# Leaving 24 unseen keys of the preceding block out of local attention, with masks made ahead of the counts

## The chip, the cores and the metric

The kernel runs on one core of one Trainium2 chip. The metric is device time in microseconds (us) of one execution. The kernel before takes 615.64 us (median of three runs, 615.52 to 617.7). The engines are called as in the profile: PE (matrix multiply; PEld is its weight load), DVE (vector), ACT (scalar), POOL, and SP, which here only issues DMA transfers.

## The reference

Attention with a local window of 96 keys, 8 global keys and a linear distance bias, followed by a feed-forward layer with a sigmoid gate. There are 4 batches of 8 heads and 768 positions, in float32.

```python
batch, n_heads, seq, head_dim = (4, 8, 768, 64);  n_global, n_local = (8, 96)
scores = scale * np.matmul(q, k.transpose(0, 1, 3, 2))
rel = pos[:, None] - pos[None, :]
is_global = pos[None, :] < int(n_global)
is_local = (rel >= 0) & (rel < int(n_local))
keep = is_global | is_local
dist = np.where(is_global & ~is_local, float(n_local), np.abs(rel).astype(np.float32))
scores = np.where(keep, scores + bias, -1000000000.0)      # bias = -slope of the head * dist
a = np.exp(scores - max);  a = a / (sum(a) + 1e-09)
x = np.matmul(a, v)                                         # to [3072 tokens, 512]
h = x @ w_in                                                # 512 -> 2048
return (h * (1.0 / (1.0 + np.exp(-1.702 * h)))) @ w_out     # 2048 -> 512
```

## The kernel before

**Blocks.** Queries are worked through in 24 blocks of 128 positions. A block's queries see keys of their own block and of the one before it, so the scores of one head are 128 x 256: 128 columns of the preceding block, then 128 of the own one. The 8 global keys are written over columns 0 to 31 (`NG = 32`) of the preceding block's keys, which are too far away for any query of this block; a mask leaves out the rest. The first block of each of the four batches (blocks 0 to 3) has no preceding one and goes another way (`first`, L555).

**A unit** (`unit`, L497) is two heads of a block: eight matmuls of 128 x 128 give the scores (L513; float32 values are carried as a high and a low half in 16 bit, hence two products for each), DVE adds the mask and takes the maximum (L519), ACT the exponential (L529), ACT and DVE split the result into halves `hl` (L533, L534), a DMA transposes them to `pt` (L535), and twelve matmuls with 64 columns multiply them with the values (L544 to L546). There are 80 units.

**The feed-forward layer** goes over 12 chunks of two blocks. Chunks 0 to 2 use plain products (L762, 128 x 256), the first two interleaved; from chunk 3 (`TWO`) on seven half products take the place of eight (L802). The products with `w_out` are L870. All 16 weight tiles (`w` followed by step and 0 for `w_in`, 1 for `w_out`) come as raw 8-byte numbers; each takes a DMA of 1 MB to one of three buffers `ws`, two ACT operations (L364, L365), two DVE (L362, L366), one ACT (L367) and one DVE (L368). Chunk 0 needs the first of them early on, so the first 80 us hold the weights, the masks and the first blocks at once.

**Masks.** `places` (POOL) writes positions, `counts` (DVE) turns n_local and n_global to numbers, `own` and `other` (DVE) make three 128 x 128 patterns `mk` out of them, and `slopes` scales each by the eight heads to `mm`: first the one for blocks 0 to 3 (task `M1`, L334 on 128 x 128), then the two for the units (`M2`, L334 on 128 x 256).

**The order of the work** is set by a planner in the kernel (`Work.order`, L94). Each task has costs by engine, tasks that it waits for, buffers from rings, and a due time; the planner goes through time and gives each free engine the ready task that is due first, not earlier than `AHEAD` us before it is due. What it writes down is the fixed sequence of each engine, SP included: engines run their own sequence in order and wait for each other by semaphores. Where PE would have nothing to do in the first `WARM` us, spare matmuls on a constant tile (`idle`, L1028) are put in. `T0`, `PACE0` and `SKEW` set the due times of chunks 0 and 1 (L900).

## Time and profile before

| what | value |
|---|---|
| three runs | 615.64 us median (615.52 to 617.7) |
| the profiled execution's own time | 614.86 us |
| its span, first to last instruction | 613.0 us |
| outside the span | 1.86 us |
| PE busy | 589.7 us (96%) |
| DVE, ACT busy | 507.5 us (83%), 485.0 us (79%) |
| granted TensorE clock, mean | 0.996 |
| DMA moved | 112.59 MB, mean 184 GB/s |

A busy PE is a modelled figure, since its matmuls overlap: each lasts longer than the time until the next one starts, so the pace is read from start to start. A view by stretches shows where PE lacks work; the waits show which engine it lacked it from; the timeline shows single instructions with their start and duration.

### The profile page before, as it was taken

To read this page: it belongs to the slowest core of one execution; us is meant where nothing else is said; L and a number is where in the kernel's file an instruction comes from. 1 tells how busy PE (TensorE), PEld (TensorE's weight loads), DVE (VectorE), ACT (ScalarE), POOL (GpSimd) and SP (SyncE) were. 2 spreads that over 40 slices of the span, in tenths; PEclk is the share of its full clock that TensorE was granted. 3 is DMA by queue.
4 is the path that set the end of the run, shared out by engine and by line. 5 is a ranking of instruction groups with operands and counts; after the bars stand their busy time and mean duration, and the time that the engine had idled before them with its cause. 6 is when DMAs were issued, how large, how long until landed. Compare 5 with 4: busy or idle time off the path is not lost.

```text
span 613.0 us, 17039 instructions
## 1 busy us (share of the span) xinstructions
PE 589.7 (96%) x6798; PEld 443.3 (72%) x6798; DVE 507.5 (83%) x1170; ACT 485.0 (79%) x1101; POOL 3.9 (1%) x16
## 2 busy tenths in 40 slices
PE   7978999999999999999999999999999999999996
PEld 4866667776776677677877668767777777867795
DVE  5699899999999999888879889879979887857533
...
GB/s 200 259 264 274 238 295 225 217 206 198 189 128 175 164 78 167 203 189 190 201 219 187 181 229 205 219 234 223 198 239 204 203 210 226 198 37 1 36 1 40
DMA packets 275670, 112.59 MB, mean 184 GB/s; under 512 B 256000, under 2 KB 256512, under 8 KB 275584
## 3 DMA queue, kind: packets, MB, share of 16 engines
...
q10 hardware_dynamic: 288, 0.00, 0.0%
HBM read 57.67 MB, written 6.29 MB: 104 GB/s over the span
## 4 chain that ended last, share of the span: by engine, by line
PE 50%; DVE 19%; DMA 12%; ACT 10%; issue 6%; SPq 1%; DVEq 0%; POOL 0%; ACTq 0%; POOLq 0%
PE y L870 22%; PE pa L802 10%; PE pb L802 7%; DMA QK<-qk 3%; DMA pt<-hl 3%; PE s L513 3%; DVE p L519 2%; ACT p L529 2%; PE h L762 2%; DVE hl L534 2%; DMA QK<-QK 2%; DVE t L772 1%; DMA ws_01again<-in_moe_w_in_dram 1%; DVE t L708 1%; ACT junk L394 1%
## 5 line engine op out<-in xcount | busy, mean ns | idle before, releaser
L870 PE MATMUL y<-w,g 128*128 128x512 f16 (+1 forms) x1248 | 268.0, 363 | 2.8 <-DVE g L774 2.0
L870 PEld LDWEIGHTS <-g 128*128 128x128 f16 x1248 | 117.7, 98 | 106.3 <-DVE g L774 3.0
L802 PEld LDWEIGHTS <-w 128*128 128x128 f16 x1728 | 101.7, 98 | 6.8 <-issue 2.1
L529 ACT ACTIVATE p<-p,NM 128x256 f32<-128x256 f32 x160 | 79.7, 501 | 6.9 <-DVE NM L519 6.7
L802 PEld LDWEIGHTS <-T 128*128 128x128 f16 x1296 | 77.0, 98 | 5.8 <-issue 0.7
L762 PE MATMUL h<-xT,w 128*128 128x256 f16 x576 | 70.1, 274 | 0.5 <-DVE w L368 0.5
L519 DVE CUSTOM_DVE_ANT_0 p<-s,mm 128x256 f32<-128x256 f32 x160 | 61.4, 420 | 7.4 <-PE s L513 6.5
L762 PEld LDWEIGHTS <-w 128*128 128x128 f16 x576 | 55.6, 99 | 10.9 <-DVE w L368 0.7
L534 DVE TENSOR_TENSOR hl<-p,hl 128x512 f16<-128x512 f32 x80 | 55.0, 688 | 9.4 <-ACT hl L533 9.0
L843 DVE SCALAR_TENSOR_TENSOR g<-t,g 128x512 f16<-128x512 f32 x72 | 49.2, 688 | 9.4 <-ACT g L842 9.0
L834 ACT ACTIVATE t<-h 128x512 f32<-128x512 f32 (+1 forms) x72 | 36.3, 518 | 24.6 <-DVE h L810 22.1
L842 ACT ACTIVATE g<-t 128x512 f16<-128x512 f32 x72 | 44.9, 629 | 9.4 <-DVE t L835 9.3
L533 ACT CAST hl<-p 128x512 f16<-128x512 f32 x80 | 49.3, 616 | 2.5 <-DMA pt<-hl 0.6
L810 DVE TENSOR_TENSOR h<-pb,h 128x256 f32<-128x256 f32 x72 | 29.5, 420 | 23.6 <-PE pb L802 20.5
L835 DVE SCALAR_TENSOR_TENSOR t<-t,h 128x512 f32<-128x512 f32 (+1 forms) x72 | 38.7, 554 | 8.1 <-ACT t L834 7.7
L802 PE MATMUL pa<-xS,T 128*128 128x128 f16 x648 | 45.0, 219 | 0.4 <-ACT h L818 0.4
L513 PEld LDWEIGHTS <-QK 128*128 128x128 f16 x640 | 39.2, 98 | 6.4 <-DVE NM L519 2.5
L513 PE MATMUL s<-QK 128*128 128x128 f16 x320 | 40.0, 219 | 0.8 <-DMA QK<-QK 0.8
L802 PE MATMUL pb<-xS,w 128*128 128x128 f16 x540 | 37.5, 219 | 1.7 <-ACT h L807 1.7
L802 PE MATMUL pa<-xT,w 128*128 128x128 f16 x540 | 37.2, 219 | 0.0
L544 PE MATMUL pv<-VR,pt 128*128 128x64 f16 x288 | 35.0, 193 | 1.1 <-DMA pt<-hl 1.1
L545 PE MATMUL pv<-VR,pt 128*128 128x64 f16 x288 | 35.0, 193 | 0.0
(184 smaller groups left out, 1076.5 us busy)
## 6 DMA issues: line engine op xcount, KB each, us to landing
...
```

The source lines that it names most:

```text
L513: nc.tensor.matmul(sp()[:, j, s * P:(s + 1) * P], d["QK"]()[:, 0, h, :], K[:, 1 + z, h, :], start=(z == 0), stop=(z == 1), skip_group_chec ...
L519: nc.vector.tensor_tensor_reduce(out=pr()[:, j, :], in0=sp()[:, j, :], in1=m, scale=-1.0 / SC, scalar=3.0e38, op0=ALU.add, op1=ALU.min, ac ...
L529: ex.append(add({"ACT": 0.28 + 0.105 * ns}, lambda e, j=j: nc.scalar.activation(pr()[:, j, :], pr()[:, j, :], AF.Exp, bias=NM[:, n, hs[j]: ...
L533: t4 = add({"ACT": 0.1 + 0.215 * ns}, lambda e: nc.scalar.copy(hl()[:, 0], pr()), ex, [pr, hl])
L534: t5 = add({"DVE": 0.07 + 0.265 * ns}, lambda e: nc.vector.tensor_sub(hl()[:, 1], pr(), hl()[:, 0]), [t4], [pr, hl])
L762: nc.tensor.matmul(ph()[:, fi, :], w1(s, cc, z, fi), X[:, y, cc, :], start=(j + cc == 0), stop=(j == 2 and cc == NCC - 1))
L802: nc.tensor.matmul(o()[:, fi], w, x()[:, y * NCC + 2 * k + cc, t], start=(first and fi + j + cc == 0), stop=(last and j + cc == 3), skip_g ...
L834: t1 = add({"ACT": 0.06 + 0.22 * w}, lambda e: nc.scalar.activation(o(), src(), AF.Tanh, scale=0.851 / (SX * SW)), after, srcs)
L835: return add({"DVE": 0.08 + 0.265 * w}, lambda e: nc.vector.scalar_tensor_tensor(o(), o(), 1.0, src(), ALU.add, ALU.mult), [t1], srcs)
L842: t4 = add({"ACT": 0.53}, lambda e, g=g, tt=tt: nc.scalar.mul(g()[:, 0], tt(), SG / (SX * SW)), u, [tt, g])
L843: t5 = add({"DVE": 0.61}, lambda e, g=g, tt=tt: nc.vector.scalar_tensor_tensor(g()[:, 1], tt(), SG / (SX * SW), g()[:, 0], ALU.mult, ALU.s ...
L870: nc.tensor.matmul(y(), part(zg, f), w2(s, z, f % 2)[:, m], start=(begin and f + j == 0), stop=(end and j == 2 and f == 2 * len(steps) - 1 ...
```

## The change

The 24 columns 0 to 23 (`SKIP = 24`) of the preceding block are left out. With 96 local keys no query sees a preceding key below column 33, so the 8 global keys now take columns 24 to 31 (`NG = 8`), and scores, masks' sum, exponential and halves work on 232 columns in place of 256. Of a unit's eight score matmuls, the four on the preceding block have 104 columns. The transpose to `pt` and the products with the values keep all 256: the two `hl` tiles are now fixed tiles, whose 24 unused columns are set to zero once (`clear`).

The copies of global keys and values are shorter, and the handover at the start of a batch copies them in place too (`lead_keys`). Masks: the part that needs no counts (`distances`) comes first, and `own` and `other` are fewer operations; the zeroing of `mT` goes from POOL to DVE. The second half of the scores of blocks 0 to 3 gets a buffer of its own kind (ring `h` in place of `s`). The planner's costs and due times are other ones.

```diff
+NG = 8
+SKIP = 24
-AHEAD = 25.0
+AHEAD = 20.0
...
-        nc.gpsimd.memset(t, 0.0)
+        nc.vector.memset(t, 0.0)
...
+    r_hl.tiles = [const.tile([P, 8 * P], F16, name=f"hl{j}") for j in range(2)]
...
+    def distances(e):
+        nc.vector.tensor_copy(flt()[:, 0:2], ints())
+        nc.vector.tensor_copy(id16, ident)
+        nc.vector.tensor_scalar(mk()[:, 1], rel(), 0.0, -BIG, ALU.is_lt, ALU.mult)
+        nc.vector.tensor_sub(mk()[:, 1], mk()[:, 1], rel())
+        nc.vector.tensor_scalar(mk()[:, 0], rel(), -1.0, float(-P), ALU.mult, ALU.add)
...
     def own(e):
-        nc.vector.tensor_scalar(nnl, nl, -1.0, None, ALU.mult)
-        nc.vector.tensor_scalar(a_(), rel(), nl, None, ALU.is_lt)
-        nc.vector.scalar_tensor_tensor(a_(), rel(), 0.0, a_(), ALU.is_ge, ALU.mult)
-        local(mk()[:, 1], 0.0)
-        nc.vector.scalar_tensor_tensor(a_(), col(), ng, a_(), ALU.is_lt, ALU.is_gt)
-        nc.vector.tensor_copy(mk()[:, 2], mk()[:, 1])
-        nc.vector.copy_predicated(mk()[:, 2], a_().bitcast(I32), nnl.broadcast_to([P, P]))
+        nc.vector.tensor_scalar(a_(), rel(), nl, -BIG, ALU.is_ge, ALU.mult)
+        nc.vector.tensor_add(mk()[:, 1], a_(), mk()[:, 1])
+        nc.vector.tensor_scalar(b_(), col(), ng, -BIG, ALU.is_ge, ALU.mult)
+        nc.vector.scalar_tensor_tensor(mk()[:, 2], b_(), nl, mk()[:, 1], ALU.subtract, ALU.max)
...
+        d["VG"] = [add({"SP": 0.3}, lambda e: nc.sync.dma_start(d["VR"]()[SKIP:SKIP + NG], d["VR"]()[0:NG]), d["v_ready"], [d["VR"]])]
...
-        W = ns * P
+        W = ns * P - SKIP
...
-                        nc.tensor.matmul(sp()[:, j, s * P:(s + 1) * P], d["QK"]()[:, 0, h, :], K[:, 1 + z, h, :],
+                        lo, hi = (0, P - SKIP) if s == 0 else (P - SKIP, W)
+                        nc.tensor.matmul(sp()[:, j, lo:hi], d["QK"]()[:, 0, h, :], K[:, 1 + z, h, P - (hi - lo):],
...
+        t4 = add({"ACT": 0.5}, lambda e: nc.scalar.copy(hl()[:, 0, :, SKIP:], pr()), ex, [pr, hl])
+        t5 = add({"DVE": 0.55}, lambda e: nc.vector.tensor_sub(hl()[:, 1, :, SKIP:], pr(), hl()[:, 0, :, SKIP:]), [t4], [pr, hl])
...
-            sp = Buf(r_s, [P, 4, P], F32, f"s{n}_{f}")
+            sp = Buf((r_s, r_h)[f], [P, 4, P], F32, f"s{n}_{f}")
...
-    T0, PACE0, PACE, PACE2, LAG, SKEW, LEAD = 20.0, 6.0, 5.9, 5.7, 16.0, 3, 68.0
+    T0, PACE0, PACE, PACE2, LAG, SKEW, LEAD = 25.0, 7.0, 5.9, 5.7, 16.0, 4, 68.0
...
-            first(n, 8.0 + 10.0 * n)
+            first(n, 8.0 + 8.0 * n)
```

Since the planner runs on these figures, the sequences of all engines move. Three places matter for the prediction.

The first is DVE at the start: `counts`, `own`, the masks of blocks 0 to 3 (`mm` 128x128 x8) and the maxima `top` of block 0. Before:

```order
L314 TENSOR_SCALAR flt_148<-flt_148,cnt_68 128x128
L315 SCALAR_TENSOR_TENSOR flt_148<-flt_148 128x128
L290 TENSOR_SCALAR flt_148<-flt_148 128x128
L291 SCALAR_TENSOR_TENSOR mk_167<-flt_148 128x128
L292 TENSOR_TENSOR mk_167<-flt_148,mk_167 128x128
L317 SCALAR_TENSOR_TENSOR flt_148<-flt_148,cnt_68 128x128
L318 COPY mk_167<-mk_167 128x128
L319 COPY_PREDICATED mk_167<-flt_148,nnl_90 128x128
L334 TENSOR_SCALAR mm_89<-mk_167 128x128 x8
```

Now:

```order
L306 SCALAR_TENSOR_TENSOR cnt_68<-cnt_68,cf_67 128x2
L319 TENSOR_SCALAR flt_123<-flt_123,cnt_68 128x128
L320 TENSOR_TENSOR mk_126<-flt_123,mk_126 128x128
L321 TENSOR_SCALAR flt_123<-flt_123,cnt_68 128x128
L322 SCALAR_TENSOR_TENSOR mk_126<-flt_123,cnt_68,mk_126 128x128
L335 TENSOR_SCALAR mm_91<-mk_126 128x128 x8
L422 TENSOR_SCALAR QZ1_133<-tq1_0_181 64x4x128
L325 TENSOR_SCALAR flt_123<-mk_126,cnt_68 128x128
L326 SCALAR_TENSOR_TENSOR mk_126<-flt_123,mk_126 128x128
L327 TENSOR_SCALAR mk_126<-flt_123,cnt_68 128x8
```

Four operations stand between the counts and the scaled mask in place of nine, three in place of seven make the other pattern, and the eight 128 x 256 scalings of the units' masks have left DVE for ACT. DVE takes over two conversions of blocks 0 and 1 from ACT (`QZ1`, and the keys of block 1).

The second is SP, after the raw weights `ws0_1`: transposes to `QK2` and `QK3` (queries and keys of blocks 2 and 3), raw weights `ws`, values `VF`. Before:

```order
L448 DMA_TRANSPOSE QK2_307<-qk162_0_270 128x16x128
L196 DMA ws1_0_335<-in_moe_w_in_dram 128x4x512
L196 DMA ws1_1_380<-in_moe_w_out_dram 128x2x1024
L450 DMA QK2_307<-QK2_307 64x1024 x2
L196 DMA ws2_0_419<-in_moe_w_in_dram 128x4x512
L448 DMA_TRANSPOSE QK3_438<-qk163_0_401 128x16x128
L431 DMA VF2_123<-in_v_dram 128x8x64
L431 DMA VF3_383<-in_v_dram 128x8x64
L196 DMA ws2_1_511<-in_moe_w_out_dram 128x2x1024
```

Now:

```order
L451 DMA_TRANSPOSE QK2_334<-qk162_0_296 128x16x128
L201 DMA ws1_0_367<-in_moe_w_in_dram 128x4x512
L201 DMA ws1_1_399<-in_moe_w_out_dram 128x2x1024
L453 DMA QK2_334<-QK2_334 64x1024 x2
L451 DMA_TRANSPOSE QK3_422<-qk163_0_406 128x16x128
L434 DMA VF2_224<-in_v_dram 128x8x64
L201 DMA ws2_0_478<-in_moe_w_in_dram 128x4x512
L453 DMA QK3_422<-QK3_422 64x1024 x2
L201 DMA ws2_1_520<-in_moe_w_out_dram 128x2x1024
```

The load of `ws2_0` has gone behind the transpose for block 3 and the values of block 2.

The third is DVE around the weight tile `w4_0`, which the fifth product of chunk 0 needs. Before:

```order
L366 ISA wa3_1_761<-wa3_1_761,w3_1_765 128x2048
L362 TENSOR_SCALAR wa4_0_827<-ws4_0_717 128x1024
L674 TENSOR_TENSOR x163_811<-x3_791,x163_811 128x512
L366 ISA wa4_0_827<-wa4_0_827,w4_0_813 128x2048
L772 SCALAR_TENSOR_TENSOR t0_3_837<-t0_3_837,h0_3_795 128x512
L368 SCALAR_TENSOR_TENSOR w3_1_765<-wa3_1_761,w3_1_765 128x1024
L446 SCALAR_TENSOR_TENSOR qk16over4_1_849<-over4_752,qk16over4_1_849 128x8x64
L368 SCALAR_TENSOR_TENSOR w4_0_813<-wa4_0_827,w4_0_813 128x1024
```

Now:

```order
L369 ISA wa3_1_758<-wa3_1_758,w3_1_740 128x2048
L369 ISA wa4_0_784<-wa4_0_784,w4_0_786 128x2048
L789 SCALAR_TENSOR_TENSOR g0_2_823<-t0_2_765,g0_2_823 128x512
L689 TENSOR_TENSOR x163_827<-x3_806,x163_827 128x512
L787 SCALAR_TENSOR_TENSOR t0_3_832<-t0_3_832,h0_3_789 128x512
L371 SCALAR_TENSOR_TENSOR w3_1_740<-wa3_1_758,w3_1_740 128x1024
L371 SCALAR_TENSOR_TENSOR w4_0_786<-wa4_0_784,w4_0_786 128x1024
L789 SCALAR_TENSOR_TENSOR g0_3_854<-t0_3_832,g0_3_854 128x512
L449 SCALAR_TENSOR_TENSOR qk164_0_845<-raw4_731,qk164_0_845 128x16x64
```

The two conversions for block 4 (`qk164` and `qk16over4`) stood ahead of `w4_0` and now stand behind it. On PE the scores of block 4's units come later as well: three of them (`s4_0`, `s4_1`, `s4_2`) now follow each other with nothing in between.

73 lines of the change are left out of this document (38 added, 35 removed).

## Prediction

> **What bounds the kernel now.** I read the stretches first, to see where PE, the busiest engine, lacks work. The columns are the stretch, its length, then busy us of PE, PEld, DVE, ACT and POOL with instruction counts, and the granted clock.
>
> ```profile
> core 0: us, PE busy (x) PEld busy (x) DVE busy (x) ACT busy (x) POOL busy (x), PEclk, DMA share, GB/s
> 0.00:20.00 20.00, 16.23 (x86) 9.64 (x87) 12.93 (x48) 8.93 (x11) 3.89 (x16) 1.00 0.90 216
> 20.00:40.00 20.00, 17.62 (x158) 15.81 (x158) 13.84 (x26) 14.71 (x16) 0.00 (x0) 0.91 1.05 255
> 40.00:60.00 20.00, 15.96 (x177) 13.20 (x175) 18.98 (x28) 17.06 (x24) 0.00 (x0) 1.00 1.02 275
> 60.00:80.00 20.00, 18.75 (x130) 12.56 (x129) 17.25 (x25) 18.10 (x24) 0.00 (x0) 1.00 1.12 254
> 80.00:140.00 60.00, 60.00 (x549) 43.31 (x548) 57.14 (x112) 57.43 (x111) 0.00 (x0) 1.00 1.08 231
> 140.00:240.00 100.00, 95.89 (x1083) 69.94 (x1082) 95.51 (x212) 80.95 (x192) 0.00 (x0) 1.00 0.83 157
> 240.00:600.00 360.00, 357.03 (x4556) 271.87 (x4554) 289.11 (x714) 285.19 (x724) 0.00 (x0) 1.00 0.87 173
> 600.00:613.00 13.00, 8.26 (x77) 6.95 (x74) 2.80 (x11) 2.65 (x7) 0.00 (x0) 0.93 0.15 47
> ```
>
> From 80 to 600 us PE is idle for 0 + 4.1 + 3.0 = 7.1 us of 520. The first 80 us hold 3.8 + 2.4 + 4.0 + 1.3 = 11.4 us of idle PE. The other engines matter where they make PE wait: in the first 80 us, and between 140 and 240 us, where DVE is busy for 95.5 of 100. So the end moves by PE's own work, by idle PE in the front, and by the 7.1 us behind it; DVE and ACT work that is saved elsewhere is hidden behind PE.
>
> That PE's busy time is its pace must be checked, since the durations overlap. The timeline shows starts (column one) and durations (column two):
>
> ```profile
> 341.27 0.19 PE L544 MATMUL pv<-VR,pt 128*128 128x64 f16 x1
> 341.30 0.19 PE L545 MATMUL pv<-VR,pt 128*128 128x64 f16 x1
> 341.32 0.19 PE L546 MATMUL pv<-VR,pt 128*128 128x64 f16 x1
> 341.35 0.28 PE L513 MATMUL s<-QK,QK 128*128 128x128 f16 x2
> 341.69 0.28 PE L513 MATMUL s<-QK 128*128 128x128 f16 x2
> 341.80 1.03 PE L870 MATMUL y<-w,g 128*128 128x512 f16 x4
> ```
>
> A matmul with 64 columns takes 0.029 us from start to start, one with 128 columns 0.056 (eight from 341.35 to 341.80). That is 0.42 ns a column and about 2 ns besides.
>
> **The change, part by part.** *Score columns.* The matmuls on the preceding block are these two groups of the view by lines, with shapes kept apart (count, then busy us and mean ns):
>
> ```profile
> L513 PE MATMUL s<-QK,QK 128*128 128x128 f16 x256 | 32.0, 219 | 1.5 <-DVE NM L519 1.3
> L513 PE MATMUL s<-QKover,QK 128*128 128x128 f16 x64 | 8.0, 219 | 0.0
> ```
>
> 320 matmuls lose 24 columns each: 320 x 24 x 0.42 ns = 3.3 us, all of it PE work and nearly all of it in the stretches where PE is never idle. The bounds are 0 (something other than the columns sets the pace) and 3.3; I take 3.3, since the 64-column rows show the pace following the columns well below 104. The Trainium skill ("TensorE: Matmul & The Clock Gate", section "Back-to-back issue gap") speaks against this: in a stream of weight loads and matmuls it has the spacing set by both, at about 81 ns for 128 columns, and by that rule shorter matmuls behind whole weight loads would save nothing. The trace does not agree: 56 ns at 128 columns and 29 ns at 64, each matmul with its load.
>
> *DVE and ACT in the units.* The same view:
>
> ```profile
> L519 DVE CUSTOM_DVE_ANT_0 p<-s,mm 128x256 f32<-128x256 f32 x160 | 61.4, 420 | 7.4 <-PE s L513 6.5
> L534 DVE TENSOR_TENSOR hl<-p,hl 128x512 f16<-128x512 f32 x80 | 55.0, 688 | 9.4 <-ACT hl L533 9.0
> L529 ACT ACTIVATE p<-p,NM 128x256 f32<-128x256 f32 x160 | 79.7, 501 | 6.9 <-DVE NM L519 6.7
> L533 ACT CAST hl<-p 128x512 f16<-128x512 f32 x80 | 49.3, 616 | 2.5 <-DMA pt<-hl 0.6
> L807 ACT COPY h<-pa 128x256 f32<-128x256 f32 x36 | 13.4, 371 | 3.1 <-PE pa L802 3.1
> ```
>
> DVE goes from 420 ns at 256 columns to 688 at 512, 1.05 ns a column: 160 x 24 + 80 x 48 columns are 7680, 8.0 us of 507. ACT by 371 and 616 is 0.96 ns a column: 7.4 us of 485. PE hides all of this from 240 us on. Between 140 and 240 us, where DVE is nearly full, there lies about a fifth of the units: 0.2 x 8.0 = 1.6 us, against 4.1 us of idle PE. I take 1.0 us off; bounds 0 and 1.6. The shorter copies of global keys and the four more small DMAs of the handovers lie far ahead of their use; I charge nothing, and 1 us if one of the handover's is late.
>
> *Masks and the first blocks.* The timeline of DVE and PE at the start, three rows of SP, and the first product of chunk 0:
>
> ```profile
> 6.51 0.69 DVE L419 TENSOR_SCALAR QZ<-tq 64x512 f32<-64x512 f32 x1 [5.55 <-ACT QZ L419]
> 7.57 0.16 DVE L297 CAST cf<-ci 128x4 f32<-128x4 int32 x1
> 8.44 0.28 DVE L314 TENSOR_SCALAR flt<-flt,cnt 128x128 f32<-128x128 f32 x1
> 8.75 0.29 DVE L315 SCALAR_TENSOR_TENSOR flt<-flt 128x128 f32<-128x128 f32 x1
> 10.65 1.17 DVE L334 TENSOR_SCALAR mm<-mk 128x128 bf16<-128x128 f32 x8
> 13.50 0.69 DVE L583 TENSOR_REDUCE top<-s 128x4 f32<-128x512 f32 x1
> 14.11 1.70 DVE L334 TENSOR_SCALAR mm<-mk 128x256 bf16<-128x256 f32 x8
> 15.83 0.69 DVE L583 TENSOR_REDUCE top<-s 128x4 f32<-128x512 f32 x1
> 16.66 0.46 PE L578 MATMUL s<-KF,QZ 128*128 128x128 f32 x2 [0.44 <-DVE top L583]
> 18.01 0.27 PE L586 MATMUL aux<-ident,top 128*8 128x128 f32 x1
> 28.21 0.38 SPq L196 DMA_DIRECT2D ws<-in_moe_w_in_dram  x1
> 33.74 3.05 SPq L448 DMA_TRANSPOSE QK<-qk  x1
> 36.84 1.95 SPq L431 DMA_DIRECT2D VF<-in_v_dram  x2
> 36.45 3.42 PE L762 MATMUL h<-xT,w 128*128 128x256 f16 x24
> ```
>
> The scaled mask of block 0 is there at 11.8 us. Now the casts and `distances` lie in DVE's 5.6 us of waiting ahead of `QZ`; behind its end at 7.2 stand four counts (0.8 us, as from 7.57 to 8.37), four 128 x 128 operations at the 0.31 of 8.44 to 8.75 (1.2) and the scaling (1.2): 10.4, 1.4 us earlier. The scores need 2 x 1.3 us (16.66 to 18.01 is one half), and the second half no longer waits for the maximum of the first; nor does the scaling of 14.11 stand ahead of its maximum. So both maxima are taken by about 13.7 in place of 16.5, and `aux` of block 0 comes at about 13.8 in place of 18.0. Behind it the same chain runs. The eight scalings on ACT, at most 8 x 0.37 = 3.0 us by the 371 ns row, start behind the other pattern at about 11.7 and end by 14.7, 0.6 us behind `aux`; ACT's 11 us of idleness in the first 20 cover them. Following block 0 and 1 with the same durations, the first product of chunk 0 comes about 4 us before 36.45.
>
> How much of this reaches the end is decided later, at the last wait for DVE before PE fills up:
>
> ```profile
> 70.10 1.22 DVE L368 SCALAR_TENSOR_TENSOR w<-wa,w 128x1024 f16<-128x1024 f32 x1
> 71.38 0.83 PE L762 MATMUL h<-xT,w 128*128 128x256 f16 x6 [0.46 <-DVE w L368]
> ```
>
> This is `w4_0`, ready at 71.3, and the second half of the fifth product of chunk 0 waiting for it. In the new sequence PE has the same work ahead of that product (the same scores, values and products of chunk 0, in another order, less what stands behind it in both). So the front gains what `w4_0` gains. Two conversions for block 4 leave DVE's queue ahead of it, one of 1024 columns, by the view by lines,
>
> ```profile
> L446 DVE SCALAR_TENSOR_TENSOR qk<-raw,qk 128x1024 f16<-128x1024 f32 x22 | 26.8, 1220 | 2.2 <-ACT qk L445 2.2
> ```
>
> and one of 512 (0.69, as `hl` above): 1.9 us. The scalings (1.7), five mask operations more than come in (at 0.31, 1.6) and a small cast (0.3) leave too, 5.5 us in all; two conversions of 0.69 like `QZ` and small fills (0.4) come in, 1.8. Net 3.7 us. Against it: the raw load of `w2_0` was issued at 28.21 and now stands behind the transpose for block 3. That was issued by 36.8 and may now be some 2 us earlier; with one load of values (1.0, half of 1.95) `w2_0` is issued at about 36, 8 us later. PE asks for it behind 5.8 us more of its own work (scores of block 3 and the first products with `w_out`), and DVE can meanwhile do other tiles, but not for all of it. I take 3.0 us for the front. The ends are 6 (the 4 us of the chain and half of the 3.7) and -5 (the late load passes on to `w4_0`).
>
> *New stalls.* `s4_0`, `s4_1` and `s4_2` follow each other directly on PE; each needs the score buffer back from two additions on DVE. The wait list of before has this wait:
>
> ```profile
> PE s L513 <- DVE NM L519: 1.3, 1, 1.3
> ```
>
> Twice 1.3 would be 2.6 us, of which the place may have some anyway by waiting for weights; I take 1.5, bounds 0 and 2.6. The fixed `hl` tiles keep the two-deep ring and so its waits.
>
> The sum on the profiled execution: 614.9 - 3.3 - 1.0 - 3.0 + 1.5 = **609.0 us** (609.1, rounded). Its 614.86 lies 0.8 below the median of 615.64, so the median could come out that much higher.
>
> **The rivals.** *The front is given back* (0.18). The late load of `w2_0` eats the 3.0 us and the stalls stay: 614.9 - 3.3 - 1.0 + 1.5 = 612.1. For it speaks that DVE and ACT are at 17 to 19 of 20 us from 40 us on; against it that DVE has less to do ahead of `w4_0`.
>
> *The columns save nothing* (0.05): 609.0 + 3.3 = 612.3. The 64-column rows speak against it. The rule of the skill named above is this one.
>
> *The front carries through* (0.08). All 6 us and no stall at `s4`: 614.9 - 3.3 - 1.0 - 6.0 = 604.6, and less than that if the half clock in the 0.91 of 20 to 40 us (0.09 x 20 = 1.8 us) goes with it.
>
> *Slower* (0.09): `w4_0` becomes the place where the program is late. PE cannot pass the fifth product of chunk 0 without it, and behind it PE has nothing idle to catch up with until 140 us. If block 3's transpose is no earlier, `w2_0` is issued at 36.8 + 1.0 = 37.8, 9.6 us late; if the ring of three raw buffers hands this on undiminished but for DVE's 3.7 us, `w4_0` is ready at 71.3 + 9.6 - 3.7 = 77.2, 5.9 later; with 2.6 of stalls: 614.9 - 3.3 + 5.9 + 2.6 = 620.1. It decides from a readiness of about 74 us on, since 71.3 + 3.3 pays for the columns. DMA at a share of 1.02 to 1.12 in that time speaks for it; that every later load (`ws3_0` on) stands earlier relative to block 4's transfers speaks against it.
>
> *The change does not do what it says* is excluded for the columns, since the new sequence has 104-column matmuls; for the masks it is the first rival.
>
> **How the numbers follow.** The forecast has 0.60. What can be told from no change in this kernel is about 0.5%, 3.1 us: faster means below 612.6, slower above 618.7. Faster: the forecast, the front that carries through, 0.10 of the first rival and 0.02 of the second: 0.80. Slower: 0.08, nearly all of the last rival. The rest, 0.12, is no difference. The range reaches from the case in which the front carries through and the clock goes with it (about 602) to past the two rivals near 612 with the median's 0.8 and 1 us for a late handover: 602 to 614.5.
>
> **What would show it.** The score matmuls on the preceding block at 0.046 us from start to start, the others at 0.056. PE's idle time from 240 to 600 us at 3 us or less. `aux` of block 0 near 14 us and the first product of chunk 0 near 32. `w4_0` ready near 68; if it is at 71 the front was given back, if beyond 74 the kernel is slower. PE waiting for DVE between `s4_0` and `s4_2`. The prediction is wrong if PE's idle time behind 80 us grows by more than 3 us, at a place that I did not name.

## The result and the profile after

The changed kernel takes 607.84 us (median of four runs, 605.45 to 609.57); the kernel before took 616.52 beside it. The ratio is 0.9849, with a 95% interval of 0.9822 to 0.9876 (the quotient of the two medians, 0.9859, lies inside it). The profiled execution has a time of 606.97 us and a span of 605.1 us, 7.9 us less than the 613.0 before. Both profiled executions are among the quicker ones of their kernels; the one before took 614.86 us, 1.7 less than the median beside the changed kernel. In the comparison of the experiments below the same kernel came out at 608.67 us, ratio 0.9878 (0.986 to 0.9897).

The view by stretches of the changed kernel, with the columns of the first view of the prediction:

```profile
core 0: us, PE busy (x) PEld busy (x) DVE busy (x) ACT busy (x) POOL busy (x), PEclk, DMA share, GB/s
0.00:20.00 20.00, 16.71 (x116) 12.20 (x117) 13.05 (x39) 10.71 (x18) 3.68 (x14) 1.00 0.97 223
20.00:40.00 20.00, 17.46 (x152) 13.64 (x152) 15.35 (x27) 14.41 (x18) 0.00 (x0) 1.00 1.00 235
40.00:60.00 20.00, 17.97 (x183) 14.31 (x181) 18.05 (x30) 18.39 (x22) 0.00 (x0) 1.00 1.04 319
60.00:80.00 20.00, 19.66 (x144) 13.75 (x143) 19.02 (x26) 20.00 (x26) 0.00 (x0) 1.00 1.00 269
80.00:140.00 60.00, 56.81 (x499) 38.72 (x497) 55.22 (x111) 51.35 (x102) 0.00 (x0) 0.97 0.99 201
140.00:240.00 100.00, 97.48 (x1141) 72.24 (x1141) 95.87 (x225) 80.14 (x192) 0.00 (x0) 1.00 0.88 157
240.00:592.00 352.00, 351.20 (x4507) 267.00 (x4505) 285.12 (x724) 276.80 (x717) 0.00 (x0) 1.00 0.88 177
```

Three things have changed. In the first 80 us PE is busy 71.8 us instead of 68.6, and the 0.91 of the clock at 20 to 40 us is gone. Between 80 and 140 us, where PE had no idle time at all, it now has 3.2 us, and a clock of 0.97. And from 140 us on it is fuller than before.

Spare matmuls and half clock hide in a busy PE. So I also counted from the starts of the matmuls: each is given 0.417 ns a column and 2.4 ns (the pace read in the prediction; float32 operands twice that), and what is left until the next start counts as time not worked, as do all spare matmuls. In us:

| profiled execution | work of PE | not worked, 0 to 80 | 80 to 140 | 140 to 240 | 240 to end | sum not worked |
|---|---|---|---|---|---|---|
| before | 566.6 | 29.1 | 0.1 | 5.2 | 5.7 | 40.1 |
| changed | 563.4 | 24.0 | 5.5 | 3.5 | 2.0 | 35.1 |
| difference | -3.2 | -5.1 | +5.4 | -1.7 | -3.7 | -5.0 |

*The front.* The timeline has these instructions: `aux` of block 0, the start of the first product of chunk 0 with its remaining 20 matmuls, and the conversion that makes `w4_0` (the second of two, ready at 64.92 + 2.35 = 67.3).

```profile
13.84 0.27 PE L602 MATMUL aux<-ident,top 128*8 128x128 f32 x1
...
30.62 0.61 PE L777 MATMUL h<-xT,w 128*128 128x256 f16 x4
32.59 2.34 PE L777 MATMUL h<-xT,w 128*128 128x256 f16 x20 [1.36 <-DVE xT L683]
...
64.92 2.35 DVE L371 SCALAR_TENSOR_TENSOR w<-wa,w 128x1024 f16<-128x1024 f32 x2
```

`aux` stood at 18.01 before, the product at 36.45, `w4_0` at 71.3.

*The units.* The view by lines, shapes kept apart (count, then busy us and mean ns):

```profile
L529 PE MATMUL s<-QK,QK 128*128 128x104 f16 x256 | 29.4, 209 | 0.7 <-DVE QK L476 0.6
L529 PE MATMUL s<-QKover,QK 128*128 128x104 f16 x64 | 7.4, 209 | 3.2 <-DVE NM L535 3.2
L535 DVE CUSTOM_DVE_ANT_0 p<-s,mm 128x232 f32<-128x232 f32 x160 | 57.6, 394 | 9.1 <-PE s L529 8.1
L550 DVE TENSOR_TENSOR hl<-p,hl 128x464 f16<-128x464 f32 x80 | 50.7, 636 | 8.0 <-ACT hl L549 7.5
L545 ACT ACTIVATE p<-p,NM 128x232 f32<-128x232 f32 x160 | 76.5, 481 | 10.9 <-DVE NM L535 10.7
L549 ACT CAST hl<-p 128x464 f16<-128x464 f32 x80 | 46.1, 576 | 1.7
```

DVE's two went from 420 to 394 ns and from 688 to 636, ACT's from 501 to 481 and from 616 to 576: 160 x 26 + 80 x 52 ns = 8.3 us less on DVE and 160 x 20 + 80 x 40 ns = 6.4 us less on ACT. All of DVE became shorter by 4.1 us only (507.5 to 503.4), ACT by 10.5: the new order gives DVE twelve operations on `x` and `yo` that ACT had, 6.1 us of DVE's time.

*The new stall.* The timeline of PE from 95 us on, with the idle time ahead of an instruction and what ended it in brackets:

```profile
95.22 0.26 PE L529 MATMUL s<-QKover,QK 128*128 128x104 f16 x2
95.31 0.28 PE L529 MATMUL s<-QK 128*128 128x128 f16 x2
95.42 0.26 PE L529 MATMUL s<-QKover,QK 128*128 128x104 f16 x2
95.52 0.28 PE L529 MATMUL s<-QK 128*128 128x128 f16 x2
96.61 0.27 PE L529 MATMUL s<-QKover,QK 128*128 128x104 f16 x2 [0.82 <-DVE NM L535]
...
99.56 0.26 PE L529 MATMUL s<-QKover,QK 128*128 128x104 f16 x2 [2.37 <-DVE NM L535]
...
99.97 4.44 PE L885 MATMUL y<-w,g 128*128 128x512 f16 x12
104.25 0.26 PE L529 MATMUL s<-QKover,QK 128*128 128x104 f16 x2
```

What DVE did in the longer gap, up to the first of the two additions of `s4_1`:

```profile
96.47 0.68 DVE L787 SCALAR_TENSOR_TENSOR t<-t,h 128x512 f32<-128x512 f32 x1
97.07 1.22 DVE L449 SCALAR_TENSOR_TENSOR qk<-raw,qk 128x1024 f16<-128x1024 f32 x1
98.21 0.39 DVE L535 CUSTOM_DVE_ANT_0 p<-s,mm 128x232 f32<-128x232 f32 x1
```

The rows of PE are `s4_0`, `s4_1`, `s4_2`, and behind twelve products `s4_3`. The first four rows give the pace: two matmuls of 104 columns take 0.09 to 0.10 us, two of 128 columns 0.10 to 0.11. Then PE stands still for 1.0 us ahead of `s4_1` and 2.5 us ahead of `s4_2`. Behind the gap the twelve products take 4.3 us from start to start, where twelve of 512 columns take 2.6 at 0.417 ns a column and 2.4 ns: the clock is at half from 100.5 to 103.9 us.

### The profile page after: what moved, and what is told of

Read it like the earlier page. It is cut to its first block, busy times and chain, and to the rows that moved or that the text cites. A ratio compares the mean times of both kernels' runs of the same rounds, so it can differ in the third digit from the quotient of the medians.

```text
span 605.1 us, 17016 instructions
## 1 busy us (share of the span) xinstructions
PE 585.4 (97%) x6802; PEld 438.9 (73%) x6802; DVE 503.4 (83%) x1177; ACT 474.5 (78%) x1096; POOL 3.7 (1%) x14
## 4 chain that ended last, share of the span: by engine, by line
PE 81%; DVE 9%; DMA 6%; issue 2%; ACT 1%; SPq 0%; DVEq 0%
PE y L885 36%; PE pa L817 15%; PE pb L817 11%; PE h L777 6%; PE s L529 5%; DMA pt<-hl 2%; PE pv L560 1%; PE pv L562 1%; PE pv L561 1%; DVE w L371 1%; PE s L594 1%; DMA QK<-qk 1%; DMA QK<-QK 1%; DMA raw<-in_k_dram 1%; DVE p L535 1%
## 5 line engine op out<-in xcount | busy, mean ns | idle before, releaser
L545 ACT ACTIVATE p<-p,NM 128x232 f32<-128x232 f32 x160 | 76.5, 481 | 10.9 <-DVE NM L535 10.7
L777 PEld LDWEIGHTS <-w 128*128 128x128 f16 x576 | 55.2, 98 | 14.0 <-issue 2.2
L535 DVE CUSTOM_DVE_ANT_0 p<-s,mm 128x232 f32<-128x232 f32 x160 | 57.6, 394 | 9.1 <-PE s L529 8.1
L550 DVE TENSOR_TENSOR hl<-p,hl 128x464 f16<-128x464 f32 x80 | 50.7, 636 | 8.0 <-ACT hl L549 7.5
L549 ACT CAST hl<-p 128x464 f16<-128x464 f32 x80 | 46.1, 576 | 1.7
L529 PEld LDWEIGHTS <-QK 128*128 128x128 f16 x640 | 36.1, 98 | 8.7 <-DVE NM L535 4.6
L529 PE MATMUL s<-QK 128*128 128x128 f16 x320 | 38.3, 219 | 0.0
```

Source lines behind the costliest of these rows:

```text
L529: nc.tensor.matmul(sp()[:, j, lo:hi], d["QK"]()[:, 0, h, :], K[:, 1 + z, h, P - (hi - lo):], start=(z == 0), stop=(z == 1), skip_group_che ...
L535: nc.vector.tensor_tensor_reduce(out=pr()[:, j, :], in0=sp()[:, j, :], in1=m, scale=-1.0 / SC, scalar=3.0e38, op0=ALU.add, op1=ALU.min, ac ...
L545: ex.append(add({"ACT": 0.473}, lambda e, j=j: nc.scalar.activation(pr()[:, j, :], pr()[:, j, :], AF.Exp, bias=NM[:, n, hs[j]:hs[j] + 1], ...
L549: t4 = add({"ACT": 0.5}, lambda e: nc.scalar.copy(hl()[:, 0, :, SKIP:], pr()), ex, [pr, hl])
L550: t5 = add({"DVE": 0.55}, lambda e: nc.vector.tensor_sub(hl()[:, 1, :, SKIP:], pr(), hl()[:, 0, :, SKIP:]), [t4], [pr, hl])
L777: nc.tensor.matmul(ph()[:, fi, :], w1(s, cc, z, fi), X[:, y, cc, :], start=(j + cc == 0), stop=(j == 2 and cc == NCC - 1))
```

## The experiments

All ratios are against the kernel before, run on the same chip beside them, with 95% intervals; 0.001 of the ratio is 0.6 us.

**The changed kernel again,** as the measure for the rest.

> The changed kernel once more, timed on the same chip as the three others of this group. Both theories: about 608 us, 8 to 9 us under the kernel before. Theory A (the gain is 3.2 us of score columns on PE, about 4 us of idle PE in the first 80 us and about 5 us of idle PE behind 140 us, less about 5 us lost between 95 and 104 us where PE waits twice for the score buffer and then runs at half clock for 3.4 us): the same wait and, in most executions, the same half clock shows in the profile again. Rival B (the half clock is an accident of one execution): PEclk is 1.00 in the stretch 80 to 140 us.

It took 608.67 us (607.68 to 610.35), ratio 0.9878 (0.986 to 0.9897). Both waits at the scores are there again, but this execution has no half clock at all ahead of the last 4 us. Its matmuls at 60 to 95 us stand 1.25 us later than in the first profile, those from 104 to 110 us 0.40 earlier: the half clock had cost 1.65 us there. By 140 us the lead is gone (0.08 later). Its span is nevertheless 0.7 us longer, by small steps of 0.1 to 0.5 us behind 270 us. So a single profile of one and the same sequence is good to about 1.5 us, and the 2.0 us of time not worked from 240 us on in the first profile was on the low side (3.5 here).

**Full columns on PE alone.** The score matmuls on the preceding block have 128 columns again; DVE and ACT still work on 232. The sequences are the same.

```diff
-        sp = Buf(r_s, [P, 2, W], F32, f"s{n}_{u}")
+        sp = Buf(r_s, [P, 2, ns * P], F32, f"s{n}_{u}")
-                        lo, hi = (0, P - SKIP) if s == 0 else (P - SKIP, W)
+                        lo, hi = s * P, (s + 1) * P
```

> The changed kernel with its four score matmuls on the preceding block back at 128 columns; the sums, exponentials and halves stay at 232 columns and every engine keeps its sequence. Theory A (PE's pace follows the columns): 320 x 10 ns = 3.2 us slower than the changed kernel, score matmuls at 0.056 us from start to start in place of 0.046. Rival C (the weight loads set the pace of short matmuls, columns save nothing): no difference, and 0.056 us in the changed kernel too.

610.41 us, ratio 0.9906 (0.9888 to 0.9924). PE's work is 566.6 us again, 3.2 more. Set against the first profile of the changed kernel, which had the same half clock, this execution falls behind evenly, from 0 at 95 us by 0.7 at 270, 1.3 at 370 and 2.1 at 430 to 2.8 at the end; between the medians the difference is 1.7 us. In this pair the columns are paid for by PE's pace, with little that hides them; the medians alone (1.7 us, each ratio good to 0.002, which is 1.2 us) leave open how much of the 3.2 us reaches the end.

**Full columns on all engines,** the same sequences.

```diff
-        W = ns * P - SKIP
+        W = ns * P
-        t4 = add({"ACT": 0.5}, lambda e: nc.scalar.copy(hl()[:, 0, :, SKIP:], pr()), ex, [pr, hl])
-        t5 = add({"DVE": 0.55}, lambda e: nc.vector.tensor_sub(hl()[:, 1, :, SKIP:], pr(), hl()[:, 0, :, SKIP:]), [t4], [pr, hl])
+        t4 = add({"ACT": 0.5}, lambda e: nc.scalar.copy(hl()[:, 0], pr()), ex, [pr, hl])
+        t5 = add({"DVE": 0.55}, lambda e: nc.vector.tensor_sub(hl()[:, 1], pr(), hl()[:, 0]), [t4], [pr, hl])
```

> The changed kernel with all 256 columns in scores, sums, exponentials and halves, sequence of every engine unchanged: what is left of the change is masks, order and due times. Against the run with wide score matmuls alone it shows what 7680 columns on DVE (8 us of work) and as many on ACT (7 us) are worth. Theory A (they are hidden behind PE; the lower idle time behind 140 us comes of the new order): 0 to 1.5 us slower than the run with wide score matmuls, idle PE from 240 us on still near 1 to 2 us. Rival D (the narrower DVE and ACT work is what took PE's idle time behind 140 us away): 4 to 5 us slower than it, idle PE from 240 us on back near 3 us.

614.06 us, ratio 0.9956 (0.994 to 0.9972): 3.65 us slower than with full columns on PE alone. The waits of PE behind 80 us, first of the kernel with full columns on PE alone, then of this one (us in total, times, longest):

```profile
PE s L529 <- DVE NM L535: 3.1, 2, 2.3
PE pv L560 <- DMA pt<-hl: 1.5, 3, 0.8
```

```profile
PE s L529 <- DVE NM L535: 4.3, 6, 2.4
PE pv L560 <- DMA pt<-hl: 3.0, 5, 1.0
```

The additions and the transposed halves come later for PE, at more places: 9.0 us of time not worked behind 140 us in place of 5.3. The time is nearer to rival D (4 to 5 us) than to theory A (0 to 1.5). In this order, then, the shorter work of DVE and ACT is worth as much as the shorter work of PE. What is left of the change without any column saved is 0.0044, 2.7 us.

**The stall filled on PE.** The 24 matmuls of `h1_3` are put between `s4_1` and `s4_2`.

```diff
+        up13 = [t for t in done if t.eng == "PE" and t in ups[1, 3]]
+        s42 = [t for t in done if t in blk[4]["S"]][2]
+        done = [t for t in done if t not in up13]
+        i = done.index(s42)
+        return done[:i] + up13 + done[i:]
```

> The changed kernel with one move in PE's sequence: the 24 matmuls of step 3 of chunk 1 (2.6 us), which stand after the sixth and seventh steps of chunk 0, go between the second and third score task of block 4, where PE waited 2.4 us. Theory A: the wait is filled (2.4 us) and PE has no reason to fall to half clock behind it (1.7 us): 3 to 4 us faster than the changed kernel. Rival E (PE then only waits later, for a weight tile or for the two result buffers that this step now takes earlier): within 1 us of the changed kernel, and a wait of 2 us or more for DVE between 100 and 115 us.

607.27 us, ratio 0.9853 (0.9833 to 0.9874): not to be told from the changed kernel, though the lower of the two, and nearest to rival E. The wait ahead of `s4_2` is gone, and others have come:

```profile
107.60 2.33 PE L885 MATMUL y<-w,g 128*128 128x512 f16 x10 [0.45 <-DVE g L789]
115.75 0.27 PE L529 MATMUL s<-QK,QK 128*128 128x104 f16 x2 [1.87 <-DVE NM L535]
```

From 80 to 140 us 4.4 us are not worked, where it was 4.4 in the second profile of the changed kernel, neither with half clock. DVE, at 55.2 of 60 us, is late in this stretch as a whole, and products that are moved only move the place where PE meets it.

**The 24 columns alone,** on the kernel before, with its masks and due times.

```diff
-NG = 32
+NG = 8
+SKIP = 24
-        W = ns * P
+        W = ns * P - SKIP
+                        lo, hi = (0, P - SKIP) if s == 0 else (P - SKIP, W)
```

> The kernel before with the 24 columns left out and nothing else; masks, due times and the front stay as they were. Theory (columns are worth 3.2 us of matrix work and some 3.7 us of shorter work on DVE and ACT, wherever the front stands): 616.9 - 3.2 - 3.7 = 610.0, ratio 0.989; the idle time of PE from 240 us to the end falls from 5.7 to about 2 us, the first product of chunk 0 stays at 36 us, w4_0 at about 71, the half clock at 34 to 38 us stays. Rival 1 (the shorter DVE and ACT work pays only together with the earlier front): 616.9 - 3.2 = 613.7, ratio 0.995, and idle time behind 240 us still near 5 us. Rival 2 (the columns are all of the change's gain): 608.7 or less, ratio 0.987.

612.98 us, ratio 0.9949 (0.993 to 0.9967): 3.1 us, PE's work alone (563.4 us). The time not worked behind 140 us went from 10.9 to 11.9 us, 3.4 of them two stretches at half clock (below). In the time the shorter work on DVE and ACT shows no gain in this order: rival 1. But without these two stretches 8.5 us would be left, 2.4 less than before, and the seven executions have granted clocks of 0.989 to 0.995, where the kernel before has 0.992 to 0.997 beside them. So it may be that the shorter work did bring something, and that the half clock took it back. Nor is this the order of before: the planner made another one for this kernel.

**The masks alone,** on the kernel before, with all 256 columns and the old due times.

```diff
-    m0 = add({"POOL": 5.3}, places, bufs=[ints])
-    m0 = add({"DVE": 1.0}, counts, [m0], [ints, flt])
+    m0 = add({"POOL": 2.0}, places, bufs=[ints], want=-9.0)
+    m0 = add({"DVE": 1.3}, distances, [m0], [ints, flt, mk], -4.0)
...
+        nc.vector.tensor_scalar(a_(), rel(), nl, -BIG, ALU.is_ge, ALU.mult)
+        nc.vector.tensor_add(mk()[:, 1], a_(), mk()[:, 1])
```

> The kernel before with the new masks alone (distances ahead of the counts, fewer operations); all 256 columns, old due times. s4_0, s4_1 and s4_2 are apart, with 6 to 24 products between them. Theory (the new masks bring the front, 4 us at w4_0, and the stall of the three scores belongs to the new order): aux of block 0 near 15 to 16, w4_0 near 68, no wait over 1 us between 80 and 140 us: 616.9 - 4 = 612.9, ratio 0.9935. Rival 1 (the front is brought by the new due times, not by the masks): w4_0 at 70 or later, 616 to 617, ratio 0.999. Rival 2 (the front's gain is taken back behind 80 us also without the three scores): w4_0 near 68 but idle time of PE from 80 us on up by 3 us or more, 616.

614.52 us, ratio 0.9965 (0.9945 to 0.9984): 2.2 us. `aux` of block 0 and the first product of chunk 0:

```profile
16.37 0.27 PE L583 MATMUL aux<-ident,top 128*8 128x128 f32 x1
...
32.52 0.61 PE L759 MATMUL h<-xT,w 128*128 128x256 f16 x4
```

So the masks make `aux` 1.6 us earlier and, with the new order that their costs give, the first product 3.9 us. There is no stall between 80 and 140 us (0.1 us not worked). But up to 80 us 29.4 us are not worked, as many as before: a stretch at half clock now lies at 55.8 to 59.2 us. And `w4_0`, which the theory had near 68, is ready at 71.7 us, no earlier than the 71.3 of before, as rival 1 had it; the time lies between the two. So the earlier first product does not travel on to `w4_0` here.

**The masks of before in the changed kernel,** all else as changed.

```diff
-    m0 = add({"POOL": 2.0}, places, bufs=[ints], want=-9.0)
-    m0 = add({"DVE": 1.3}, distances, [m0], [ints, flt, mk], -4.0)
+    m0 = add({"POOL": 5.3}, places, bufs=[ints])
+    m0 = add({"DVE": 1.0}, counts, [m0], [ints, flt])
...
-        nc.vector.tensor_scalar(a_(), rel(), nl, -BIG, ALU.is_ge, ALU.mult)
-        nc.vector.tensor_add(mk()[:, 1], a_(), mk()[:, 1])
+        nc.vector.tensor_scalar(nnl, nl, -1.0, None, ALU.mult)
+        nc.vector.tensor_scalar(a_(), rel(), nl, None, ALU.is_lt)
```

> The changed kernel with the masks of the kernel before (counts first, all operations behind them); the 24 columns, the due times and the second score buffer of the first blocks as changed. s4_0, s4_1 and s4_2 are then apart, with 6 to 12 products between them. Theory (the masks set the front, and the front reaches the end): the first product of chunk 0 comes 3 to 4 us later than in the changed kernel (34 to 35 in place of 30.6), the idle time of PE up to 80 us rises by 3 us or more, the stall of 3.6 us at the scores is absent: 608.3 + 3.5 - 3.6 = 608.2, ratio 0.986 to 0.988. Rival 1 (the masks bring nothing that reaches the end; the order does): front as early as in the changed kernel by 80 us, 604.7, ratio 0.981. Rival 2 (as with the old due times, another stall takes the place): 612 or more, with a wait of 2 us or more between 80 and 240 us.

610.32 us, ratio 0.9876 (0.985 to 0.9903), the changed kernel's 0.9878. The front of this kernel:

```profile
16.96 0.27 PE L604 MATMUL aux<-ident,top 128*8 128x128 f32 x1
...
31.07 0.61 PE L779 MATMUL h<-xT,w 128*128 128x256 f16 x4
32.63 2.34 PE L779 MATMUL h<-xT,w 128*128 128x256 f16 x20 [0.95 <-DVE xT L685]
```

`aux` is 3.1 us later than in the changed kernel, but the first product starts 0.45 us later, and its second part, which waits for `xT`, at the same time (32.63 and 32.59). The earlier masks of block 0 do not travel on to chunk 0. What does must lie in the order, in which block 1 is due 8 us behind block 0 in place of 10, the second half of the scores has a ring of its own, and the product stands ahead of the scores of block 2. The kernel with the old due times (below), with 10 us in place of 8, has the first product at 31.27 us as well, so the 8 us are not needed for it; the one with the masks alone, without the ring, has it at 32.52. No run takes these three apart one at a time. Up to 80 us 2.4 us more are not worked than in the changed kernel (26.4), part of them a half clock at 41.2 to 44.6 us; `w4_0` is ready at 70.3 us. The three scores are apart in this order and there is no stall; from 240 us on, however, 9.2 us are not worked, about half of them in waits for the transposed halves (the row has all behind 80 us; 4.5 of the 5.9 us lie behind 240):

```profile
PE pv L562 <- DMA pt<-hl: 5.9, 7, 1.4
```

So the ratio came out as the theory has it, but by other parts: 2.4 us in the front (1.1 against the second profile), and new waits in place of the stall, none of them as long as the 2 us of rival 2, and most of them later than it said.

**Columns and masks with the old due times.**

```diff
-AHEAD = 20.0
+AHEAD = 25.0
-    T0, PACE0, PACE, PACE2, LAG, SKEW, LEAD = 25.0, 7.0, 5.9, 5.7, 16.0, 4, 68.0
+    T0, PACE0, PACE, PACE2, LAG, SKEW, LEAD = 20.0, 6.0, 5.9, 5.7, 16.0, 3, 68.0
-            first(n, 8.0 + 8.0 * n)
+            first(n, 8.0 + 10.0 * n)
```

> The changed kernel with the due times and the look-ahead of the kernel before; columns and masks as changed. s4_0, s4_1 and s4_2 then have 12, 12 and 24 products between them. Theory (the 3.6 us stall belongs to the new order alone): idle time of PE from 80 to 140 us 1.5 us or less in place of 5.5, front as in the changed kernel (w4_0 at 67 to 69): 608.2 - 3.6 - 0.8 (half clock in some executions) = 603.8, ratio 0.979. Rival 1 (as with the moved products, DVE is late there whatever the order, and the wait only moves): 607 to 608.5, ratio 0.985 to 0.987, with waits of 3 us or more for DVE between 80 and 240 us. Rival 2 (the new due times bring the front): w4_0 at 70 or later, 610 or more.

614.49 us (610.77 to 617.73), ratio 0.9969 (0.9951 to 0.9987). The theory falls. The front is as early (first product at 31.27), and the scores are apart; but at the same time stands a worse stall, with other work. The timeline of PE:

```profile
95.96 0.20 PE L560 MATMUL pv<-VRover,pt 128*128 128x64 f16 x1 [2.16 <-DMA pt<-hl]
...
99.91 4.33 PE L777 MATMUL h<-xT,w 128*128 128x256 f16 x22 [3.42 <-DVE t L787]
```

From 93.3 us on DVE does conversions of weights (four), one of a block and one of halves ahead of the `t` for which PE waits. With the half clock, 8.1 us are not worked from 80 to 140 us. The new due times are thus worth 0.009 (5.6 us) where columns and masks are there already, hardly by the front (25.0 us not worked up to 80 us, 24.0 in the changed kernel), but by how PE and DVE meet around 95 us. Rival 2 has its signs (`w4_0` at 72.3 us, and over 610), but not its cause: the front is early all the same. And the profiled execution is one of the two quickest: these two have a granted clock of 0.994 and took 610.8 and 610.9 us, the ten others 0.984 to 0.991 and 613.9 to 617.7.

**The same once more, for its profile.**

> The kernel with the columns and masks of the change and the old due times once more, for its profile: the first profiled execution took 610.9, the others mostly 614 to 615. Theory (the difference is half clock): an execution of 614 to 615 shows two stretches of 3.413 us at half clock more than the two of the first profile, each behind a stretch with under 0.40 of PE work. Rival (the front): the first product of chunk 0 or w4_0 comes 3 us later. Rival (many small waits): idle time behind 140 us up by 3 us with no more half clock.

612.09 us, 1.2 more than the first profiled execution. It has three stretches at half clock, one more than the first, at the same stall, and 9.9 us not worked from 80 to 140 us. That agrees with the theory. No execution of 614 to 615 was profiled, but the granted clocks of the ten above agree too: a stretch at half clock takes 0.0028 off the mean clock (1.7 of 610 us), so the 0.006 that they have less on average is about two stretches, 3.7 of the 4.2 us that they took longer.

**Spare matmuls in the gap.** Ten matmuls of 512 columns, whose result nobody uses, right ahead of `s4_2`.

```diff
+        s42 = [t for t in done if t in blk[4]["S"]][2]
+        z = Buf(r_h, [P, 4 * P], F32, "idleh")
+        t = Task({"PE": 2.2}, lambda e: [nc.tensor.matmul(z(), idle[:, 0:P], idle, start=True, stop=True) for _ in range(10)], (), [z], 0.0)
+        t.eng = "PE"
+        i = done.index(s42)
+        return done[:i] + [t] + done[i:]
```

> The changed kernel with ten spare matmuls of 512 columns (2.2 us, thrown away) right ahead of s4_2, in the gap in which PE waits for DVE. Theory (the half clock of 3.4 us behind the gap is set off by the gap, in some executions): granted clock 1.00 from 80 to 140 us, s4_2 at the same time as without them to 0.3 us, and a time of 607 or a little less, with all executions near the lowest: 0.8 us below the changed kernel's median on average, 1.7 in the executions that had the half clock. Rival 1 (the half clock comes whatever PE does there): the clock of that stretch stays near 0.97 and the time near 608.5. Rival 2 (the spare matmuls reach past DVE's result and hold up s4_2): the time rises by up to 1 us.

609.55 us, ratio 0.9882 (0.9863 to 0.9901): no gain. From 80 to 140 us the clock is 1.00, and PE was 1.56 us ahead of the first profile of the changed kernel from 104 to 115 us, which is the price of the half clock. At 143.38 us it then waited 1.88 us for a transposed tile, and there the half clock came after all. So the gap sets it off, as the theory says, and in this execution filling one gap did not free it of the next. It is not typical, though: its granted clock is 0.994, that of the five others 0.998 to 1.0. These had next to no half clock, and took 607.7 to 610.8 us all the same. As the theory has it the half clock went, but the time did not follow.

**DVE's additions of `s4_1` ahead** of a multiplication of chunk 0 and the conversion for block 5:

```diff
+        S = blk[4]["S"]
+        for u in (1,):
+            rows = [t for t in done if t in checks and t in S[u].next]
+            i = max(done.index(a) for r in rows for a in r.after) + 1
+            done = [t for t in done if t not in rows]
+            done = done[:i] + rows + done[i:]
```

> The changed kernel with one thing reordered on DVE: the two additions of s4_1 (the rows p<-s,mm) stand ahead of the multiplication of product chunk 0 (t<-t,h) and the conversion for block 5 (qk<-raw,qk) that were ahead of them. Theory 1 (s4_2 waits for those two operations): PE's wait ahead of s4_2 falls from 2.6 to about 0.8 us, so the stall from 3.6 to 1.8. Theory 2 (the half clock: PE's time is cut into stretches of 3.413 us, and behind every one in which PE worked for less than 0.40 of it, the next is at half clock; so in all ten profiles so far, with 0.39 the highest that was followed and 0.40 the lowest that was not): the two stretches at the scores hold at least 0.47 of work wherever the cuts fall, and no half clock appears between 80 and 140 us. Time 608.2 - 1.8 - 0.9 = 605.5, ratio 0.982. Rival (the wait only moves, as with the moved products): PE waits as much for the multiplication or the conversion some 5 to 15 us later, 607.5 to 608.5.

609.2 us, ratio 0.9886 (0.9857 to 0.9914): no gain. Theory 1 and 2 hold at the place: ahead of `s4_2` the bracket has 0.8 us (1.0 of standing still, as ahead of `s4_1`) in place of 2.4 (2.5), and there is no half clock. But right behind, PE waits for what was put back, and later for transfers:

```profile
97.94 0.27 PE L529 MATMUL s<-QKover,QK 128*128 128x104 f16 x2 [0.82 <-DVE NM L535]
99.20 0.60 PE L885 MATMUL y<-w,g 128*128 128x512 f16 x2 [0.68 <-ACT g L788]
100.83 2.33 PE L885 MATMUL y<-w,g 128*128 128x512 f16 x10 [1.02 <-DVE g L789]
...
357.55 0.23 PE L529 MATMUL s<-QK 128*128 128x128 f16 x1 [0.96 <-DMA QK<-QK]
```

From 80 to 140 us 4.5 us are not worked: the rival.

**Both: additions ahead, and `h1_3` in between.**

```diff
+        for u in (1,):
+            rows = [t for t in done if t in checks and t in S[u].next]
...
+        up13 = [t for t in done if t.eng == "PE" and t in ups[1, 3]]
+        i = done.index(S[2])
+        done = done[:i] + up13 + done[i:]
```

> Both reorderings: the additions of s4_1 ahead on DVE, and the 24 matmuls of h1_3 between s4_1 and s4_2 on PE. Theory 1: the stall at the scores is the 1.0 us ahead of s4_1 alone; with the products moved alone PE waited later, 0.8 us at 107 and 2.3 us at 113, for g behind the delayed multiplication, and these remain: 607.3 - 0 to 1. Theory 2 (the half clock follows a stretch of 3.413 us with under 0.40 of work): none between 80 and 140 us, unless the wait at 113 falls into one stretch (0.40 there before). Rival (DVE has now slack at both places): 604.5, ratio 0.980.

608.7 us, ratio 0.9873 (0.9845 to 0.9901): no gain either. The 24 products wait themselves, at 99.36 us and for 1.42 us, for the multiplication (`t`) that was put back; 4.6 us are not worked from 80 to 140 us.

No version beats the changed kernel by more than the measurement can tell. The time not worked in all profiles, counted as in the table above (us; the ten spare matmuls in the gap count as not worked too), with the half clock of all executions in the last column:

| kernel | 0 to 80 | 80 to 140 | 140 to 240 | 240 to end | behind 80 | ratio | half clock |
|---|---|---|---|---|---|---|---|
| changed, second time | 25.3 | 4.4 | 3.3 | 3.5 | 11.2 | 0.9878 | 2.2 |
| full columns on PE | 24.0 | 5.4 | 3.0 | 2.3 | 10.7 | 0.9906 | 2.8 |
| full columns on all | 25.1 | 5.1 | 4.1 | 4.9 | 14.1 | 0.9956 | 2.5 |
| stall filled | 24.4 | 4.4 | 3.5 | 4.0 | 11.9 | 0.9853 | 1.4 |
| spare matmuls | 24.1 | 4.4 | 4.9 | 4.7 | 13.9 | 0.9882 | 0.8 |
| additions ahead | 24.0 | 4.5 | 3.8 | 5.2 | 13.5 | 0.9886 | 2.5 |
| both | 24.8 | 4.6 | 3.4 | 4.1 | 12.1 | 0.9873 | 0.9 |
| masks of before | 26.4 | 1.2 | 2.5 | 9.2 | 12.9 | 0.9876 | 2.3 |
| old due times | 25.0 | 8.1 | 2.2 | 3.6 | 13.9 | 0.9969 | 6.8 |
| old due times, again | 25.6 | 9.9 | 0.8 | 4.1 | 14.7 | | 6.1 |
| columns alone | 28.0 | 1.2 | 4.3 | 7.6 | 13.1 | 0.9949 | 5.1 |
| masks alone | 29.4 | 0.1 | 5.4 | 5.6 | 11.1 | 0.9965 | 1.9 |

The last column is an estimate: one minus the granted clock of an execution, times its span, as the mean of all executions of the kernel (of one alone for the one without a ratio). The kernel before has 2.7 to 3.3 beside them. It includes half clock at the very end, where PE has no work left, so a difference under 1 us says nothing. With the old due times it is 4.6 us more than in the changed kernel the second time, most of the 5.6 us; with the masks alone it is 1.4 us less than in the kernel before beside it, which may be much of their 2.2 us. But the kernels with spare matmuls and with both moves have next to none of it and are no faster than the changed one.

## The half clock

In ten of the fourteen profiles at least one stretch of 3.41 us at half clock turned up ahead of the kernel's end, at changing places. All changes of the granted clock within one execution lie whole multiples of 3.413 us apart, so PE's time can be cut there. Three cuts at the scores in the first profile of the changed kernel (length, PE busy, granted clock):

```profile
93.67:97.09 3.42, 2.60 (x30) 1.00 1.05 350
97.09:100.50 3.41, 1.04 (x13) 1.00 0.85 142
100.50:103.91 3.41, 3.41 (x10) 0.50 1.24 121
```

The same gap in the second profile of the same kernel:

```profile
95.88:99.29 3.41, 1.74 (x23) 1.00 1.17 308
99.29:102.70 3.41, 1.89 (x15) 1.00 0.77 133
```

The gap is the same, but here a cut falls into it, so that neither piece is empty enough, and the clock stays. Where the cuts lie differs: they start between 4.0 and 7.2 us in the fourteen profiles. With spare matmuls in that gap, the wait at 143 us:

```profile
140.94:144.35 3.41, 1.53 (x30) 1.00 1.21 117
144.35:147.76 3.41, 3.41 (x12) 0.50 1.18 239
```

And in the kernel with the columns alone, where two small waits each put PE into half clock:

```profile
376.31:379.73 3.42, 1.05 (x17) 1.00 1.18 188
379.73:383.14 3.41, 3.41 (x42) 0.50 0.89 185
```

Over all fourteen profiles, 2,455 stretches ahead of the kernel's end: of those at full clock, the eleven with PE busy for 1.53 us or less were all followed by one at half clock. At 1.54 one was not, at 1.56 one was, and from 1.6 us on none was. So the half clock follows a stretch in which PE is busy for less than about 0.45 of its 3.413 us, and costs up to 1.7 us at its place; a gap of 2.5 us can be enough or not, by where it lies. (Counted by work from the starts, as the expectations do, the border is less sharp and near 0.40: the fullest stretch that was followed has 0.39, the emptiest that was not 0.38.) The Trainium skill ("TensorE: Matmul & The Clock Gate", "Part 1: The HAM clock gate", on what happens) has a free-running window of 3413 ns, which these profiles agree with. It has the clock fall after an idle window; here a window with 1.53 us of work was enough.

## Why the prediction was right, and where it was not

The forecast was 609.0 us on the profiled execution, -5.9 of its 614.9 (its terms add up to -5.8); it came to 606.97, -7.9, and the median to 607.84. That it came so near is in part luck: the front brought 2.1 us more than its term, the stall cost 3.9 more than its term, and the waits behind 140 us fell by 4.4 more than their term, so that the last two errors cancel. Term by term:

*Score columns, -3.3.* Right (320 x 24 x 0.42 ns is 3.2): 566.6 to 563.4 us of work, the spacing 0.046 us, and 2.8 us in the pair of profiles with the same sequence (1.7 between medians). The section of the Trainium skill that was weighed there ("TensorE: Matmul & The Clock Gate", "Back-to-back issue gap") has the spacing at about 81 ns for 128 columns and 131 ns for 512; here it is 56 ns at 128 and 46 ns at 104, and the measurement decides. That the columns would save nothing was the prediction's reading of it: its two figures give, as an estimate, 0.13 ns a column, 1.0 us in all.

*DVE and ACT, -1.0.* The mechanism was there, the place wrong. The step that failed is "PE hides all of this from 240 us on": with full columns on these engines, the changed order loses 3.65 us, at additions and transposed halves all along, 240 us and later included. PE is busy for 351.2 of 352 us there because these come just in time. With the columns alone, in the order that the planner makes then, the same saving shows nothing in the time, with the half clock as a possible reason. So a size for this term is not to be had from the profile of before alone; my upper bound of 1.6 took the stretch in which PE was idle in one order for the only one in which the work counts.

*The front, -3.0.* The points that I named came: `aux` at 13.84 (13.8), `w4_0` at 67.3 (68), the first product at 30.6 (32, even earlier). In time not worked the front gained 5.1 us (3.8 by the second profile), up to 1.7 of it the half clock that lay there before. But the step "Behind it the same chain runs", which carried the earlier masks to the first product, failed: with the masks of before in the changed order `aux` is 3.1 us later and that product 0.45. The order brings most of it, and without the new masks the changed kernel is not measurably slower (0.9876 and 0.9878, each good to 0.002 or 0.003). Nor does the step "So the front gains what `w4_0` gains" hold in general: with the old due times `w4_0` comes 0.9 us later than before, and yet 4.1 us less are not worked up to 80 us. The late load of `w2_0`, which was to make it slower, did not decide.

*New stalls, +1.5.* Named at the right place, for the right reason, and mis-sized: 3.5 us of waiting, and 1.65 of half clock where the cuts fall badly. The row that I took for a price (1.3 us a wait) was what was left of a wait behind twelve products of PE, which hid 1.3 us of it (139.3 to 140.6 us before); here PE had nothing in between, and DVE had a multiplication and a conversion of 1.22 us ahead of the additions. Against this stands what I did not expect either: taking the wait ahead of `s4_2` away or shortening it, in three ways, and its half clock in a fourth (next to none in five of six executions), brought nothing that can be measured.

*The sum behind 80 us.* In the first profiles 11.0 us are not worked behind 80 us before, and 11.1 after: what the stall cost came in from shorter waits later (-1.7 and -3.7). The kernels with the changed order and its columns have 11.1 to 13.9, whatever was done at the scores. The change as measured is then the front and the columns: -5.1 - 3.2 = -8.3 against a span shorter by 7.9. Why PE's later waits grow when the stall is taken away, whether because it arrives earlier at DVE's and the DMA's work or by the variation between executions (1.5 us), is not settled.

*The parts do not add.* With all parts the ratio is 0.9849 and 0.9878 in two comparisons. The columns alone give 0.9949, the masks alone 0.9965, both with the old due times 0.9969 (much of the difference half clock), the columns with the new due times 0.9876, masks and new due times without the columns 0.9956. What was common to the good ones is columns and due times together.
